# Eight of 28 row blocks of a down product moved from TensorE to ScalarE and GpSimd, and four weight loads asked for eight steps earlier

## Chip, cores and metric

One core of a Trainium2 chip. The metric is the device time of one execution in microseconds (us). The three timed runs of the kernel before took 263.06, 263.49 and 263.74 us; their median, 263.49 us, is the time to compare with. About 0.3% (0.79 us) is what a measurement of this kernel can tell from no change.

## The reference

The output mixes two branches of one input `x` (2048 tokens of 1024 columns, bf16) by a gate per token.

```python
g = sigmoid((x * gate_w).sum(-1, keepdims=True))
# branch a: linear attention, 32 heads of 32 columns, over all tokens
q, k, v = split(x @ wqkv)
phi(z)  = concat(softmax(z @ w_phi), softmax(-(z @ w_phi)))     # per head
kv, z   = sum over tokens of phi(k)^T v,  and of phi(k)
a       = (phi(q) kv / (phi(q) z + 1e-6)) @ wo
# branch b: one expert, for one token only
idx     = argmax over tokens of x @ w_r
y       = (silu(x[idx] @ w_gate) * (x[idx] @ w_up)) @ w_down    # 1024 -> 3584 -> 1024
b       = x, with y * sigmoid(r[idx]) added to row idx
out     = g * a + (1 - g) * b
```

The last product of branch b, (1 x 3584) @ (3584 x 1024), is the down product. 3584 rows are 28 blocks of 128.

## The kernel before

TensorE works through three stages. First v of all 16 token tiles, with the folding of `w_phi` into the k and q weights. Then a loop of steps `i`: steps 0 to 31 are the key stage, one half of the heads of one token tile a step (`feats` computes pk, two exponentials on ScalarE, `ssum` and its reciprocal `rq` on VectorE, the product `phi` on GpSimd, and `k_kv`, five steps later, adds to `kvps`). Steps 32 to 63 (NU = 32) are the query stage: `feats` gives `pq` and `phi`; `q_turn` transposes `phi` by DMA into `phT`; `q_num` later multiplies it with KV (`num`), and VectorE divides (`rden`, `o_sb`); `q_oT` transposes by DMA into `oT`; `q_wo` later multiplies by `wo` (`po`), and VectorE combines with `xg` into `oo`, which is stored. How much later is set by a running count of TensorE's time, `pe`: a step takes what is due.

The one token of branch b is worked in between. Its weights pass through SBUF in 1 MB buffers: "A" is one of three in the pool `ring`, "D" one of two in `shp`, "W" and "V" halves of a tile in `wob`, "X" and "Y" halves of one in `w16`. The up and gate products take four passes r (`ffn_gu`): passes 0 and 1 at step 14, passes 2 and 3 at step 22. `gu_load` asks for a buffer of weights; in pass 1 each buffer takes two DMAs, a gate part of 768 KB and an up part of 256 KB. Pass 0 is asked for at step 0 (`gu0`), the others where they are used. At steps 4 and 7 `qfold_turn` issues four DMA transposes each (`wqf` from `wfT`); the `ring` buffer of the first `wfT` is the one that the last buffer of pass 1 takes over.

At step 38 (DN) `ffn_down` loads the down weights (seven chunks of four row blocks) and issues 56 matmuls into one PSUM bank, `yps`: 28 blocks times two column halves, in four column groups of 32 that run side by side. `moe_cols` copies the bank out and gathers four rows into `y4` (8 x 2 x 128) by four small DMAs. `moe_sum` (step 44) adds the two parts on GpSimd into `y2`, `moe_scale` (46) scales it, `moe_out` (47) writes it to DRAM (`ydr`), and `moe_spread` (57), held to program order, reads it back broadcast over 128 partitions (`ybc`). Tiles 14 and 15 add `ybc` in `q_xg`; for the others `add_row` adds the row in DRAM.

A compiler puts instructions in order on each engine and in each DMA queue, by the program's order and by what it holds to be ready; what is wrapped in `keep_in_program_order` stays in the order written. Each engine then runs its list in order.

Of the kernel before, what the change touches and what calls it, by code (L numbers as in the profile page):

```python
# [9 lines left out]
F32 = mybir.dt.float32  # L10
I32 = mybir.dt.int32
U32 = mybir.dt.uint32
ALU = mybir.AluOpType
ACTF = mybir.ActivationFunctionType
AX = mybir.AxisListType
# [3 lines left out]
P = 128  # L19
# [15 lines left out]
VC = [0, 256, 640, 1026]  # L35
VW = 1026
TOH = 14
TX = 4
KFOLDS = {5: (0, 3), 7: (3, 3), 9: (6, 2)}
PACKS = {(13, 2): (0, 0), (14, 1): (1, 0), (15, 0): (0, 1), (15, 2): (1, 1)}  # L40
# [130 lines left out]
def kernel(  # L171
# [74 lines left out]
    nc.gpsimd.iota(iot[:, 0:NT], pattern=[[1, NT]], base=0, channel_multiplier=0, allow_small_or_imprecise_dtypes=True)  # L246
    nc.gpsimd.iota(iot[:, NT:NT + 1], pattern=[[0, 1]], base=0, channel_multiplier=1, allow_small_or_imprecise_dtypes=True)
    hh = const.tile([P, NFB], BF, name="hh")

    small_ps = psS.tile([P, 512], F32, name="small_ps")  # L250
    ffn_ps = small_ps[:, 0:64]
# [272 lines left out]
        return w  # L524

    def ffn_gu(r, bufs):
        ws = moe.pop("gu0", None) or [gu_load(r, k, b) for k, b in enumerate(bufs)]
        acc = psB.tile([P, 512], F32, name="facc", tag="pB")
        for k, w in enumerate(ws):
            for q in range(2):  # L530
                for g in range(4):
                    kb = 4 * k + 2 * q + g // 2 if r == 3 else 2 * k + q
                    nc.tensor.matmul(acc[32 * g:32 * g + 32, :], lhsT=xs32[:, kb, :],  # L533
                                     rhs=w[:, (q * 4 + g) * 512:(q * 4 + g + 1) * 512], start=(k == 0 and q == 0),
                                     stop=(k == len(ws) - 1 and q == 1),
                                     tile_position=(0, 32 * g), skip_group_check=True)
        gs = wk.tile([P, 512], F32, name="gs", tag="junk", bufs=2)
        nc.scalar.copy(out=gs[:], in_=acc[:])
        g0 = 16 * r
        step = 4 if r >= 1 else 1  # L540
        for g in range(0, 4, step):
            nc.sync.dma_start(out=gT[g0 + 4 * g:g0 + 4 * (g + step), :], in_=gs[32 * g:32 * (g + step):32, :])

    def ffn_down(c0, c1):
        if c0 == 0:
            moe["wd"] = [wd_load(c, p) for c, p in enumerate("AAADDWV")]
            moe["yps"] = psB.tile([P, 512], F32, name="yps", tag="pB")
        ws = moe["wd"]
        for blk in range(4 * c0, 4 * c1):
            for n in range(2):  # L550
                g = (blk % 2) * 2 + n
                nc.tensor.matmul(moe["yps"][32 * g:32 * g + 32, :], lhsT=hh32[:, blk, :],  # L552
                                 rhs=ws[blk // 4][:, blk % 4, n * 512:(n + 1) * 512], start=(blk < 2),
                                 stop=(blk >= NFB - 2), tile_position=(0, 32 * g), skip_group_check=True)

    def moe_cols():
        ym = ring.tile([P, D * 2], F32, name="ym", tag="wch")
        ys = ym[:, 0:512]
        y4 = ym[0:KB, 512:768].rearrange("p (s c) -> p s c", s=2)
        ybc = ym[:, 1280:1792].bitcast(BF)  # L560
        moe["ybc"] = ybc
        nc.scalar.copy(out=ys, in_=moe["yps"][:])
        for g in range(4):
            nc.sync.dma_start(out=y4[4 * (g % 2):4 * (g % 2) + 4, g // 2, :], in_=ys[32 * g:32 * g + 1, :])
        moe["y4"] = y4

    def moe_sum(tick):
        y4 = moe["y4"]
        y2 = const.tile([KB, P], BF, name="y2")
        moe["y2"] = y2  # L570
        nc.gpsimd.tensor_copy(out=y2[0:1, 0:1], in_=tick)
        nc.gpsimd.tensor_tensor(out=y2[:], in0=y4[:, 0, :], in1=y4[:, 1, :], op=ALU.add)

    def moe_scale(tick):
        y2 = moe["y2"]
# [228 lines left out]
    GU = (14, 22)  # L804
    TU = 29
    DN = NU + 6
    TF, TNUM, TWO, TKV = 1.73, 0.27, 1.73, 0.27
    L_NUM0, N_1, L_NUM1, L_NUM, L_WO0, L_WO, MOST = 11.0, 6, 17.0, 11.5, 8, 6, 2
    pe = 0.0
# [4 lines left out]
    while i < 2 * NU or n_next < NU or wos:  # L814
        if i in GU:
            r = 2 * GU.index(i)
            ffn_gu(r, 'WVAD')
            ffn_gu(r + 1, ('DXYA', 'AA')[r // 2])
        if i == DN - 3:
            nc.scalar.copy(out=hh32[0:1, 0, 0:1], in_=moe["e"][0:1, 0, 1, 0:1])  # L820
            nc.scalar.copy(out=hh32[:], in_=hh[:].unsqueeze(2).to_broadcast([P, NFB, 32]))
        if i == 19:
            moe["wo"] = w16.tile([P, KB, D], BF, name="wo_sb", tag="w16")
            nc.gpsimd.tensor_copy(out=moe["wo"][0:1, 0, 0:1], in_=kst[i - 1][0:1, 0, 0, 0:1])
            nc.sync.dma_start(out=moe["wo"][:], in_=A_wo.rearrange("(kb p) n -> p kb n", p=P))
        if i == DN:
            ffn_down(0, 7)
            moe_cols()
            qp["oo"] = wob.tile([P, 16, 512], BF, name="oo", tag="wo")
            qp["n_oo"] = 0  # L830
            qp["late"] = []
        if LAG <= i < NU + LAG:
            k_kv(i - LAG)
            pe += TKV
        if i < NU:
            kst[i] = feats(i, wkf, False)
        if i == NU:
            qp["phT"] = wfp.tile([P, 8, NPU, P], BF, name="phT", tag="wf")
        if i == NU + LAG - 1:
            kv_finish()  # L840
            kscope.close()
            kvscope.close()
            psN = main.enter_context(tc.tile_pool(name="psN", bufs=1, space=PSUM))
            qp["num"] = [psN.tile([P, 2 * 512], F32, name="num%d" % h_) for h_ in range(2)]
            qp["qw"] = main.enter_context(tc.tile_pool(name="qw", bufs=2))
        if NU <= i < 2 * NU:
            q_turn(i - NU, feats(i - NU, wqf, True))
            pe += TF
            fend[i - NU] = pe
        if i == 0:  # L850
            moe["gu0"] = [gu_load(0, k, b) for k, b in enumerate("WVAD")]
        if i < 4:
            kv_zero(i)
        if i == 2:
            gates()
        if i in (QT0, QT1):
            h = 4 * (i == QT1)
            nc.scalar.copy(out=wqf[0:1, 0, h * P:(h + 4) * P:P], in_=moe["e"][0:1, 0, 0, 0:4])
            for a in range(h, h + 4):
                qfold_turn(a)  # L860
        if i == TU:
            ffn_turn()
            ffn_mid()
        if i == 0:
            route_row()
        if i == 10:
            xs_turn()
        if i == 16:
            one_hot()
        if i == 19:  # L870
            one_hot_cols()
        if i == 23:
            one_hot_sums()
        if i == NU + 18:
            one_hot_row()
        if i == DN + 6:
            moe_sum(moe["rs"][0:1, 0:1])
        if i == DN + 8:
            moe_scale(moe["rs"][0:1, 0:1])
        if i == DN + 9:  # L880
            moe_out()
        if i == DN + 19:
            moe_spread()
        late = i >= 2 * NU
        for k in range(MOST if not late else 1):
            if n_next >= NU or n_next not in fend or pe < fend[n_next] + (L_NUM0 if n_next < N_1 else max(L_NUM, L_NUM1 - 1.5 * max(0, n_next - 26))):
                break
            q_num(n_next)
            pe += TNUM
            nend[n_next] = pe  # L890
            if n_next % 2 == 1:
                q_oT(n_next // 2)
                wos += [(n_next // 2, 0), (n_next // 2, 1)]
            n_next += 1
            if n_next == NU:
                range_flag()
                flag_in = 1
        wo_at = nend[2 * wos[0][0] + 1] + (L_WO if wos[0][0] else L_WO0) if wos else 1e9
        if late and pe < wo_at:
            pe = min(wo_at, fend[n_next] + L_NUM if n_next < NU else 1e9)  # L900
        if pe >= wo_at:
            t, nh = wos.pop(0)
            if nh == 0:
                q_xg(t)
            q_store(0 if late else 1)
            q_wo(t, nh, late and nh == 1)
            if t == NT - 1:
                q_store(0)
            if (t, nh) == (NT - 2, 1):
                tc.mark_branch_hint_location("general", engines=[ET.PE])  # L910
            pe += TWO
            if n_next == NU:
                flag_in -= 1
                if flag_in == 0:
                    range_flag_end()
            if (t, nh) == (TOH - 1, 1):
                q_store(0)
                add_row(moe["y2c"][:, 0, :], nc.values_load(moe["ixu"][0:1, 0:1], engines=[ET.Pool], min_val=0,
                                                            max_val=TOH * P - 1))
        i += 1  # L920
# [40 lines left out]
```

## Time and profile before

| | |
|---|---|
| median of the timed runs | 263.49 us |
| the profiled execution | 264.23 us |
| its span, first to last instruction | 262.6 us |
| TensorE (PE) busy | 256.4 us |
| VectorE (DVE) busy | 175.4 us |
| GpSimd (POOL) busy | 128.1 us |
| ScalarE (ACT) busy | 127.6 us |
| clock granted to TensorE | 0.999 of full speed |

The durations below come from the profiled execution, which took 0.74 us more than the median; its span leaves out 1.63 us around the first and the last instruction. A line such as "L552 PE MATMUL yps<-wch,hh x56" reads: line 552 of the kernel, engine, operation, what is written from what, how many. Matmuls are pipelined, and the profile models where one ends, so the distance from the first matmul of a group to the first of the next is the better measure of what a group takes.

### The profile page before, as it was taken

To read this page: it belongs to the slowest core of one execution; us is meant where nothing else is said; L and a number is where in the kernel's file an instruction comes from. 1 tells how busy PE (TensorE), PEld (TensorE's weight loads), DVE (VectorE), ACT (ScalarE), POOL (GpSimd) and SP (SyncE) were. 2 spreads that over 40 slices of the span, in tenths; PEclk is the share of its full clock that TensorE was granted. 3 is DMA by queue.
4 is the path that set the end of the run, shared out by engine and by line. 5 is a ranking of instruction groups with operands and counts; after the bars stand their busy time and mean duration, and the time that the engine had idled before them with its cause. 6 is when DMAs were issued, how large, how long until landed. Compare 5 with 4: busy or idle time off the path is not lost.

```text
span 262.6 us, 5420 instructions
## 1 busy us (share of the span) xinstructions
PE 256.4 (98%) x2039; PEld 137.9 (53%) x2062; DVE 175.4 (67%) x310; ACT 127.6 (49%) x262; POOL 128.1 (49%) x87
## 2 busy tenths in 40 slices
PE   7999999999999999999999999999999999999995
PEld 3666666665445545545555455445444444445543
DVE  3020221015879855998798769899799797888973
ACT  3043555447575544545556667447344553435220
POOL 6000000000079995779989868665535545455001
PEclk9999999999999999999999999999999999999999
DMA  6979999988999889969995998999977899999962
GB/s 203 279 129 176 167 198 150 196 122 309 408 384 182 192 210 386 401 199 391 386 387 184 195 151 178 236 169 250 250 168 155 171 180 177 206 190 206 141 164 83
DMA packets 111082, 58.48 MB, mean 223 GB/s; under 512 B 93692, under 2 KB 98892, under 8 KB 111052
## 3 DMA queue, kind: packets, MB, share of 16 engines
q1 hardware_dynamic: 108364, 53.77, 85.8%
q10 hardware_dynamic: 2656, 4.33, 6.9%
q8 instruction: 17, 0.28, 0.5%
q14 instruction: 13, 0.11, 0.2%
q0 software_dynamic: 32, 0.00, 0.1%
HBM read 31.27 MB, written 4.23 MB: 135 GB/s over the span
## 4 chain that ended last, share of the span: by engine, by line
PE 96%; DMA 2%; issue 1%; SPq 0%; DVE 0%
PE pq L645 21%; PE pk L645 21%; PE po L747 21%; PE pv L599 19%; PE kvps L675 3%; PE num L708 3%; PE facc L533 3%; DMA wv_sb<-in_A_wqkv_dram 2%; PE vbank L616 1%; PE pv L616 1%; PE yps L552 1%; PE vbank L323 1%; PE vbank L340 1%; SPq L273 0%; PE pW L323 0%
## 5 line engine op out<-in xcount | busy, mean ns | idle before, releaser
L662 POOL TENSOR_TENSOR phi<-e,rq 128x1024 bf16<-128x1024 bf16 x64 | 121.4, 1912 | 61.7 <-DVE rq L659 36.0
L655 DVE TENSOR_REDUCE ssum<-e 128x32 f32<-128x1024 bf16 x64 | 77.4, 1210 | 14.3 <-ACT e L651 14.0
L645 PEld LDWEIGHTS <-xT 128*128 128x128 bf16 x512 | 47.4, 98 | 51.9 <-issue 0.7
L645 PE MATMUL pq<-wqf,xT 128*128 128x512 bf16 x256 | 60.3, 379 | 0.0
L645 PE MATMUL pk<-wkf,xT 128*128 128x512 bf16 x245 | 59.2, 379 | 0.6
L747 PE MATMUL po<-wo_sb,oT 128*128 128x512 bf16 (+2 forms) x252 | 58.1, 372 | 0.6
L599 PE MATMUL pv<-wv_sb,xT 128*128 128x256 bf16 (+2 forms) x336 | 50.0, 307 | 0.0
L599 PEld LDWEIGHTS <-xT 128*128 128x128 bf16 x336 | 32.0, 97 | 16.3 <-issue 0.5
L607 ACT CAST v_all<-pv 128x384 bf16<-128x384 f32 (+1 forms) x45 | 20.1, 451 | 34.9 <-PE pv L599 25.7
L747 PEld LDWEIGHTS <-oT 128*128 128x128 bf16 x264 | 24.0, 98 | 23.9 <-issue 0.2
L650 ACT ACTIVATE e<-pq 128x512 bf16<-128x512 f32 x32 | 18.9, 592 | 34.2 <-PE pq L645 34.2
L650 ACT ACTIVATE e<-pk 128x512 bf16<-128x512 f32 x32 | 19.1, 597 | 26.3 <-PE pk L645 22.1
L475 POOL COPY wch<-shv 1x1 bf16<-1x1 bf16 x3 | 0.4, 177 | 53.4 <-DMA shv<-in_A_wqkv_dram 53.4
L751 DVE SCALAR_TENSOR_TENSOR oo<-po,gate,xg 128x512 bf16<-128x512 f32 (+2 forms) x33 | 23.8, 722 | 3.6 <-PE po L747 3.5
L659 DVE RECIPROCAL rq<-ssum 128x32 f32<-128x32 f32 x64 | 22.2, 347 | 1.3
L713 DVE TENSOR_TENSOR o_sb<-num,rden 128x512 bf16<-128x512 f32 x32 | 21.7, 679 | 0.7
L328 DVE CAST wkf<-vbank 128x512 bf16<-128x512 f32 x6 | 3.9, 686 | 25.2 <-PE vbank L323 25.2
L651 ACT ACTIVATE e<-pk 128x512 bf16<-128x512 f32 x32 | 18.9, 591 | 0.0
L651 ACT ACTIVATE e<-pq 128x512 bf16<-128x512 f32 x32 | 18.9, 590 | 0.0
L732 ACT ACTIVATE xg<-xin,omg 128x1024 f32<-128x1024 bf16 x16 | 18.4, 1148 | 0.5
L346 DVE CAST wfT<-vbank 128x512 bf16<-128x512 f32 x9 | 5.8, 681 | 16.5 <-PE pW L340 16.5
L675 PEld LDWEIGHTS <-phi 128*128 128x128 bf16 x256 | 12.0, 98 | 7.3 <-issue 0.8
(137 smaller groups left out, 154.0 us busy)
## 6 DMA issues: line engine op xcount, KB each, us to landing
wch<-in_B_w_down_dram SPq DMA_DIRECT2D x7, 1024.0 KB
wch<-in_B_w_up_dram SPq DMA_DIRECT2D x6, 1024.0 KB
wch<-in_B_w_gate_dram SPq DMA_DIRECT2D x4, 1024.0 KB
xin<-in_A_x_dram ACTq DMA_DIRECT2D x16, 256.0 KB
out_dram<-oo SPq DMA_DIRECT2D x31, 128.0 KB
wch<-in_B_w_gate_dram SPq DMA_DIRECT2D x4, 768.0 KB
wv_sb<-in_A_wqkv_dram SPq DMA_DIRECT2D x8, 256.0 KB
wo_sb<-in_A_wo_dram SPq DMA_DIRECT2D x1, 2048.0 KB
```

Source lines behind the costliest of these rows:

```text
L599: nc.tensor.matmul(pv[:, 0:hi - lo], lhsT=xT[:, kb, t * P:(t + 1) * P], rhs=wv_sb[:, kb, lo:hi], start=(kb == 0), stop=(kb == KB - 1))
L607: copy(out=v_all[:, t, h0:h1, 0:DH], in_=pv[:, 0:(h1 - h0) * DH].rearrange("p (h d) -> p h d", d=DH))
L645: nc.tensor.matmul(pk[:].rearrange("p (c r) f -> p c r f", r=4) if is_q else pkf, lhsT=xT[:, kb, t * P:(t + 1) * P], rhs=q_heads(wf, kb, h ...
L650: nc.scalar.activation(out=e[:, :, 0, :], in_=pk[:], func=ACTF.Exp)
L651: nc.scalar.activation(out=e[:, :, 1, :], in_=pk[:], func=ACTF.Exp, scale=-1.0)
L655: nc.vector.tensor_reduce(out=ssum[:], in_=e2, axis=AX.X, op=ALU.add)
L659: nc.vector.reciprocal(out=rs, in_=ssum[:])
L662: nc.gpsimd.tensor_tensor(out=phi[:].rearrange("p h s f -> p (h s) f"), in0=e2, in1=_bc(rs, [P, HH * 2, DH]), op=ALU.mult)
L675: nc.tensor.matmul(kv_slot(pr), lhsT=phi[:, 2 * pl:2 * pl + 2, :, :].rearrange("p h s f -> p (h s f)"), rhs=v_all[:, t, hf * HH + 2 * pl:h ...
L713: nc.vector.tensor_tensor(out=st["o"][:, hf * HH:(hf + 1) * HH, :].rearrange("p (r h) d -> p r h d", h=2), in0=nv[:, :, :, 0:DH], in1=rden ...
L747: nc.tensor.matmul(po[:, 0:w], lhsT=st["oT"][:, kb, :], rhs=moe["wo"][:, kb, sl], start=(kb == 0), stop=(kb == KB - 1))
L751: qp["gated"] = nc.vector.scalar_tensor_tensor(out=o_out[:, 0:w], in0=po[:, 0:w], scalar=gate[:, t:t + 1], in1=st["xg"][:, sl], op0=ALU.mu ...
```

## The change

Eight of the 28 blocks of the down product, chunks 1 and 2, are no longer multiplied on TensorE. `down_part` runs from step 44 on, one or two parts a step, sixteen in all (eight blocks times two column halves): ScalarE multiplies a 128x512 piece of the weights by the block's column of `hh` (kept in f32 as `hhf`), and from the third part on GpSimd adds the piece into an f32 accumulator `acc` of 128x1024. At step 56 `down_cols` sums `acc` over its partitions on VectorE with a transpose in blocks of 32, a reduction and a second transpose; at step 57 four DMAs put the four partial sums next to the two from TensorE. `moe_sum` moves from GpSimd to VectorE and from step 44 to 59, `moe_scale` from 46 to 60, `moe_out` from 47 to 61, `moe_spread` from 57 to 63. The loads of the down weights come in another order and other buffers: chunks 0, 3, 4, 5, 6 for TensorE first, then 1 and 2. The loads of pass 1 of the up and gate weights are written at step 6 instead of step 14.

```diff
+PW = (1, 2)
+    hhf = const.tile([P, NFB], F32, name="hhf")
     def ffn_gu(r, bufs):
-        ws = moe.pop("gu0", None) or [gu_load(r, k, b) for k, b in enumerate(bufs)]
+        ws = moe.pop("gu%d" % r, None) or [gu_load(r, k, b) for k, b in enumerate(bufs)]
...
-    def ffn_down(c0, c1):
-        if c0 == 0:
-            moe["wd"] = [wd_load(c, p) for c, p in enumerate("AAADDWV")]
-            moe["yps"] = psB.tile([P, 512], F32, name="yps", tag="pB")
-        ws = moe["wd"]
-        for blk in range(4 * c0, 4 * c1):
+    def ffn_down():
+        moe["wd"] = {c: wd_load(c, p) for c, p in zip((0, 3, 4, 5, 6) + PW, "ADDWVAA")}
+        moe["yps"] = psB.tile([P, 512], F32, name="yps", tag="pB")
+        blks = [b for b in range(NFB) if b // 4 not in PW]
+        for blk in blks:
             for n in range(2):
                 g = (blk % 2) * 2 + n
                 nc.tensor.matmul(moe["yps"][32 * g:32 * g + 32, :], lhsT=hh32[:, blk, :],
...
+    def down_part(n):
+        b, half = divmod(n, 2)
+        blk = 4 * PW[b // 4] + b % 4
+        if n == 0:
+            moe["acc"] = qp["qw"].tile([P, D], F32, name="acc", tag="acc", bufs=1)
+        o = moe["acc"][:, half * 512:(half + 1) * 512]
+        w = moe["wd"][PW[b // 4]][:, b % 4, half * 512:(half + 1) * 512]
+        to = o if b == 0 else qp["qw"].tile([P, 512], F32, name="prod", tag="prod", bufs=2)[:]
+        tc.keep_in_program_order(nc.scalar.activation(out=to, in_=w, func=ACTF.Copy, scale=hhf[:, blk:blk + 1]))
+        if b:
+            tc.keep_in_program_order(nc.gpsimd.tensor_tensor(out=o, in0=to, in1=o, op=ALU.add))
+
+    def down_cols():
+        tr = ring.tile([P, D * 2], F32, name="tr", tag="wch")
+        tc.keep_in_program_order(nc.vector.transpose(out=tr[:, 0:D], in_=moe["acc"][:]))
+        nc.vector.tensor_reduce(out=tr[:, D:D + 32], in_=tr[:, 0:D].rearrange("p (c i) -> p c i", i=32), axis=AX.X, op=ALU.add)
+        nc.vector.transpose(out=tr[:, D + 32:D + 64], in_=tr[:, D:D + 32])
+        moe["part"] = tr[:, D + 32:D + 64]
+
+    def down_gather():
+        for q in range(4):
+            nc.sync.dma_start(out=moe["y4"][:, 2 + q, :], in_=moe["part"][32 * q:32 * q + 32, :])
...
-        nc.gpsimd.tensor_copy(out=y2[0:1, 0:1], in_=tick)
-        nc.gpsimd.tensor_tensor(out=y2[:], in0=y4[:, 0, :], in1=y4[:, 1, :], op=ALU.add)
+        nc.vector.tensor_copy(out=y2[0:1, 0:1], in_=tick)
+        with nc.allow_low_precision(reason="fp32 sum, rounded once"):
+            nc.vector.tensor_reduce(out=y2[:], in_=y4.rearrange("p s c -> p c s"), axis=AX.X, op=ALU.add)
...
+    DP = DN + 6
...
             nc.scalar.copy(out=hh32[:], in_=hh[:].unsqueeze(2).to_broadcast([P, NFB, 32]))
+            nc.scalar.copy(out=hhf[:], in_=hh[:])
...
+        if i == QT1 - 1:
+            moe["gu1"] = [gu_load(1, k, b) for k, b in enumerate("DXYA")]
...
-        if i == DN + 6:
+        if DP <= i < DP + 11:
+            for n in range((i - DP) * 3 // 2, (i - DP + 1) * 3 // 2):
+                down_part(n)
+        if i == DP + 12:
+            down_cols()
+        if i == DP + 13:
+            down_gather()
+        if i == DP + 15:
             moe_sum(moe["rs"][0:1, 0:1])
-        if i == DN + 8:
+        if i == DP + 16:
             moe_scale(moe["rs"][0:1, 0:1])
-        if i == DN + 9:
+        if i == DP + 17:
             moe_out()
-        if i == DN + 19:
+        if i == 2 * NU - 1:
             moe_spread()
```

## Rows read from the trace of the kernel before

**Rows 1.** The page, part 1: span, and TensorE's busy time.
```profile
span 262.6 us, 5420 instructions
...
PE 256.4 (98%) x2039; PEld 137.9 (53%) x2062; DVE 175.4 (67%) x310; ACT 127.6 (49%) x262; POOL 128.1 (49%) x87
```

**Rows 2.** All that TensorE's matmuls waited for: us in total, times, longest us.
```profile
PE small_ps L207 <- PEq L945: 1.1, 1, 1.1
PE vbank L616 <- DMA wv_sb<-in_A_wqkv_dram: 0.8, 1, 0.8
```

**Rows 3.** Two stretches: length, busy us (instructions) of PE, PEld, DVE, ACT, POOL; clock, DMA.
```profile
168.00:210.00 42.00, 41.74 (x280) 20.85 (x284) 37.31 (x65) 20.13 (x37) 21.93 (x14) 1.00 0.93 197
...
212.00:238.00 26.00, 25.84 (x167) 12.73 (x168) 21.51 (x37) 11.93 (x22) 14.01 (x8) 1.00 0.97 183
```

**Rows 4.** Instructions in time, down product on TensorE: start us, length us, which.
```profile
147.76 3.21 PE L552 MATMUL yps<-wch,hh 128*32 128x512 bf16 x56
150.90 1.47 PE L645 MATMUL pq<-wqf,xT 128*128 128x512 bf16 x6
```

**Rows 5.** Instructions in time, up and gate passes on TensorE.
```profile
93.40 4.01 PE L533 MATMUL facc<-wch,xs 128*32 128x512 bf16 x64
...
96.82 0.10 PEld L533 LDWEIGHTS <-xs 128*32 128x32 bf16 x4 [0.50 <-issue]
...
97.34 0.43 PE L675 MATMUL kvps<-v_all,phi 128*128 128x66 bf16 x8
...
113.32 2.77 PE L533 MATMUL facc<-wch,xs 128*32 128x512 bf16 x48
...
116.02 0.43 PE L675 MATMUL kvps<-v_all,phi 128*128 128x66 bf16 x8
```

**Rows 6.** Instructions in time, SyncE's queue ahead of the first passes.
```profile
85.97 0.41 SPq L509 DMA_DIRECT2D wch<-in_B_w_gate_dram  x1
86.49 7.00 SPq L349 DMA_TRANSPOSE wqf<-wfT  x4
93.54 2.81 SPq L509 DMA_DIRECT2D wch<-in_B_w_up_dram  x3
```

**Rows 7.** Groups by line and shape: count | busy us, mean ns of one | idle before.
```profile
L662 POOL TENSOR_TENSOR phi<-e,rq 128x1024 bf16<-128x1024 bf16 x64 | 121.4, 1912 | 61.7 <-DVE rq L659 36.0 <-ACT e L651 12.5 <-DVE rden L712 5.7
L655 DVE TENSOR_REDUCE ssum<-e 128x32 f32<-128x1024 bf16 x64 | 77.4, 1210 | 14.3 <-ACT e L651 14.0
...
L732 ACT ACTIVATE xg<-xin,omg 128x1024 f32<-128x1024 bf16 x16 | 18.4, 1148 | 0.5
...
L572 POOL TENSOR_TENSOR y<-ym 8x128 bf16<-8x128 f32 x1 | 0.4, 446 | 0.1
...
L571 POOL CAST y<-rq 1x1 bf16<-1x1 f32 x1 | 0.2, 176 | 0.0
```

**Rows 8.** Instructions in time, VectorE and TensorE around step 50.
```profile
191.26 0.74 DVE L751 SCALAR_TENSOR_TENSOR oo<-po,gate,xg 128x512 bf16<-128x512 f32 x1
...
192.65 1.67 DVE L450 TENSOR_TENSOR ixm<-ixm,ixf 1x1 f32<-1x1 f32 x1
...
194.42 0.23 DVE L712 RECIPROCAL rden<-num 128x16 f32<-128x16 f32 x1
...
196.42 1.89 PE L747 MATMUL po<-wo_sb,oT 128*128 128x512 bf16 x7
```

**Rows 9.** Instructions in time: an output transpose, and the matmuls that read it.
```profile
222.43 1.24 SPq L723 DMA_TRANSPOSE oT<-o_sb  x1
...
237.21 1.67 PE L747 MATMUL po<-wo_sb,oT 128*128 128x512 bf16 x7
```

**Rows 10.** Instructions in time: gather, last query transpose, reader of the spread row.
```profile
155.70 2.95 SPq L564 DMA_DIRECT2D ym<-ym  x4
...
243.21 1.24 SPq L692 DMA_TRANSPOSE phT<-phi  x1
...
247.73 1.28 DVE L734 SCALAR_TENSOR_TENSOR xg<-ym,oh,xg 128x1024 f32<-128x1024 bf16 x1
```

More of the change, by code (lines that the diff above doesn't have):

```diff
@@ L552, in ffn_down @@
                 nc.tensor.matmul(moe["yps"][32 * g:32 * g + 32, :], lhsT=hh32[:, blk, :],
-                                 rhs=ws[blk // 4][:, blk % 4, n * 512:(n + 1) * 512], start=(blk < 2),
-                                 stop=(blk >= NFB - 2), tile_position=(0, 32 * g), skip_group_check=True)
+                                 rhs=moe["wd"][blk // 4][:, blk % 4, n * 512:(n + 1) * 512], start=(blk < 2),
+                                 stop=(blk in blks[-2:]), tile_position=(0, 32 * g), skip_group_check=True)
+    def down_part(n):
[18 more added lines that the diff above has]
+            nc.sync.dma_start(out=moe["y4"][:, 2 + q, :], in_=moe["part"][32 * q:32 * q + 32, :])
     def moe_cols():
@@ L558, in moe_cols @@
         ys = ym[:, 0:512]
-        y4 = ym[0:KB, 512:768].rearrange("p (s c) -> p s c", s=2)
+        y4 = ym[0:KB, 512:1280].rearrange("p (s c) -> p s c", s=6)
         ybc = ym[:, 1280:1792].bitcast(BF)
@@ L826 @@
         if i == DN:
-            ffn_down(0, 7)
+            ffn_down()
             moe_cols()
```

## The prediction

> **What bounds the kernel now.** I read the page's first part, then what TensorE waited for, then the stretches of the stage that the change loads. TensorE is busy for 256.4 of the 262.6 us span [rows 1], and its waits for others come to 1.9 us, both at the start [rows 2]. So a matmul taken off it is worth its time, and work on another engine costs nothing until TensorE has to wait for it. From 168 to 210 us VectorE is busy 37.3 of 42 us, ScalarE 20.1 and GpSimd 21.9 [rows 3]: VectorE is the one with little room.
>
> **The down product.** The 56 matmuls of `yps` begin at 147.76 us, the next `pq` at 150.90 [rows 4]: 3.14 us, 56.1 ns each. The change leaves 40 (16 of 56 go, two per block). Four neighbouring column groups stay in the same rotation, since the blocks that go are an even count in a row. Saved: 16 x 56.1 ns = **0.90 us**, straight from the path. The seven loads keep their size; only the order and the buffers change, and the two chunks for ScalarE sit in two `ring` buffers until used.
>
> **The experts' second weights.** The 64 matmuls of passes 0 and 1 begin at 93.40 us and are followed by `kvps` at 97.34: 3.94 us. The 48 of passes 2 and 3 take 113.32 to 116.02: 2.70 us, 56.25 ns each. At that rate 64 take 3.60, so 0.34 us is a stall, and the weight loads stand still before the last four of them at 96.82 [rows 5]. The reason is in SyncE's queue: the gate part of the last buffer of pass 1 is asked for at 85.97, then come four transposes of `wqf` from 86.49 to 93.49, and only then the up part of the same buffer (the first of three at 93.54) [rows 6]. Nothing in TensorE's list of waits names it [rows 2], because a matmul in flight is drawn busy until its modelled end. With the load written at step 6, ahead of those transposes (step 7), both parts should go at about 86 us. The transposes then come one issue (about 0.5 us) later; what they write is first read by `pq` in the query stage, which begins six steps ahead of the down product at 147.76 [rows 4], so some 40 us hide it. Gain: between 0 (the compiler's order keeps the up part behind the transposes) and 0.34 us; I take **0.34**, because the gate part already overtook those transposes with a later step number.
>
> **ScalarE's products.** 16 multiplications of 128x512 bf16 into f32. Not in the trace; the nearest is `xg`, the same operation on 1024 columns, 1148 ns [rows 7]. Between half of it and all of it; I take 0.6 us: 9.6 us in all, against 21.9 us that ScalarE is free in the stretch [rows 3]. On the path: 0.
>
> **GpSimd's sums.** 14 f32 additions of 128x512 (the first product of each half goes straight into `acc`). Nearest rows: `phi`, 1912 ns for 1024 columns; the small sum `y`, 446 ns for 128 columns of two f32 inputs; and 176 ns for a single element [rows 7]. By columns of `phi` one addition takes 0.96 us. From `y`, (446 - 176) / 128 = 2.1 ns a column, it takes 512 x 2.1 + 176 = 1.26 us. By bytes of `phi` (2 KB read and 2 KB written per partition in 1.74 us, where the addition reads 4 KB and writes 2) it takes 2.8 us. I take 1.26, the one row of the same kind: 14 x 1.26 = 17.6 us. GpSimd is free for 42 - 21.9 = 20.1 us in the stretch, and the two `y` instructions that leave it give 0.6 more: it fits, at 95% of the engine. The end at 2.8 us is a rival below.
>
> The Trainium skill, page "GPSIMD Engine Reference", section "Elementwise — side-by-side cycle accounting", speaks against putting such additions on GpSimd and gives 4497 ns for 2048 f32 columns. Scaled to 512 columns that is an estimate of 1.12 us, 15.7 us for all; by that page the sum above would be the same, and the price by bytes would be out.
>
> What hides a late GpSimd: it runs `phi`, whose transpose is consumed far later. The same distance shows in the output: the eleventh `oT` transpose is issued at 222.43 us and the po group that reads it (the 21st of 32) begins at 237.21 [rows 9]. So delays of a few us on either chain reach nobody. The short distances are buffers: one `oo` ends at 192.0 and the `po` after next begins at 196.42 [rows 8], 4.4 us of slack; the two `pq` buffers, freed by ScalarE's exponentials, turn in the same rhythm, with about as much.
>
> A wait is added on ScalarE: each product waits for the addition two before it (two `prod` buffers), and the next exponentials queue behind it, for which `pq` waits. It holds TensorE only once GpSimd is more than those 4.4 us behind.
>
> **VectorE's new work, steps 56 to 59 (about 209 to 226 us).** A 128x1024 f32 transpose, a reduction of 1024 columns, a 32-column transpose, a 768-column reduction in place of GpSimd's sum. Nearest row: `ssum`, 1024 columns in 1210 ns [rows 7]. I take 1.2 + 1.2 + 0.1 + 0.9 = 3.4 us; 2.2 if the transpose costs nothing, 4.6 if it costs double. VectorE is free for 26 - 21.5 = 4.5 us between 212 and 238 [rows 3]. The trace has such a burst already: at step 50 four `ixm` instructions (1.67 us the longest) push the next `rden` to 194.42 with no idle time ahead of it, and the `po` at 196.42 begins on time [rows 8]. The burst at step 56 is some 0.4 us longer and comes at the same place in the rhythm. On the path: 0, up to 1.2 us if the dear end meets a late gather.
>
> **SyncE's queue.** The gather at step 57 adds four small DMAs. The four of `moe_cols` took 2.95 us of issue [rows 10]; behind them stand `phT`, `oT` and stores, with the distances above. Row `ydr` is written at step 61 instead of 47. The spread moves from step 57 to 63 and, pinned, comes after the last `phT` at 243.21; its consumer in VectorE's order stands at 247.73 [rows 10]. That leaves some 3 us for 256 KB: tight, but the two tiles that read the result close only the last four of 32 outputs. On the path: 0 to 0.5 us. The extra copy `hhf` lies on ScalarE ahead of the query stage: nothing.
>
> **Sum.** The profiled execution took 264.23 us (span 262.6 and 1.63 around it), 0.74 above the median of 263.49. 264.23 - 0.90 - 0.34 = 262.99; on the median, 263.49 - 1.24 = **262.25 us**.
>
> **Rivals.**
> (a) The order of the loads does not change what TensorE sees: the up part stays behind the transposes. Then only the down product counts: 263.49 - 0.90 = 262.6 us. For it: the order on SyncE is the compiler's, and it mixed the steps before. Against: the new step number is below that of the transposes.
> (b) The new work at the end of the query stage collides: VectorE's dear end, a sum that waits at the head of its queue for the gather, and the late spread cost TensorE 0.5 to 1.2 us: 262.75 to 263.45 us. For it: VectorE has 4.5 us left for 3.4. Against: 4.4 us of slack at the buffers, and the burst at step 50.
> (c) Slower: GpSimd's additions go by bytes, 2.8 us each. 14 x 2.8 = 39.2 us against 20.7 free: 18.5 us too many; the buffers swallow 4.4, the rest reaches TensorE by way of ScalarE: 263.49 - 1.24 + 14.1 = 276 us. It loses more than 0.3% once an addition takes over 1.94 us (14 x 1.94 = 27.1 = 20.7 + 4.4 + the gain of 1.24 + 0.8). Against: by bytes the small `y` sum would take 0.73 us, and it takes 0.45.
>
> **How the numbers follow.** Forecast 0.62, (a) 0.15, (b) 0.17, (c) 0.06. 0.3% is 0.79 us, about what a measurement of this kernel can tell from no change: faster means below 262.70. The forecast holds there with some 0.59 of its 0.62 (three runs of before lie within 0.43 of their median), (a) with 0.09 of its 0.15; (b) is nearly all within 0.3%. So faster 0.68, same 0.25, slower 0.07. Low end: the forecast less the spread of runs, 261.85; high end: the dear end of (b), 263.4; what is left out is (c) and edges.
>
> **What would show it.** Right: 40 `yps` matmuls in 2.25 us; passes 0 and 1 in 3.60 us, with both parts of the last buffer issued next to each other near 86 us; `po` and `pq` at 3.71 us a pair through 168 to 238 us; POOL near 95% busy from 168 to 205. Wrong: a wait of TensorE for VectorE or ScalarE anywhere after 165 us, additions over 1.9 us, or the exponentials waiting behind products.

## The result and the profile after

The changed kernel is slower: 267.4 us (266.95 to 268.14) against 263.69 us for the kernel before in runs beside it, ratio 1.0132, 95% interval 1.0101 to 1.0162. The prediction was 262.25 us, faster. Its profiled execution took 267.97 us, with a span of 266.3.

Read first what the forecast promised. Page of the changed kernel, part 1 (answers [rows 1]):

```profile
PE 256.9 (96%) x2046; PEld 137.6 (52%) x2046; DVE 176.7 (66%) x315; ACT 137.8 (52%) x279; POOL 144.6 (54%) x99
```

Instructions in time on TensorE, changed kernel: start us, length us (answers [rows 4, 5]):

```profile
93.66 3.64 PE L535 MATMUL facc<-wch,xs 128*32 128x512 bf16 x64
97.23 0.43 PE L700 MATMUL kvps<-v_all,phi 128*128 128x66 bf16 x8
...
147.65 2.34 PE L553 MATMUL yps<-wch,hh 128*32 128x512 bf16 x40
149.92 1.25 PE L670 MATMUL pq<-wqf,xT 128*128 128x512 bf16 x5
```

The down product takes 149.92 - 147.65 = 2.27 us in place of 3.14, passes 0 and 1 take 97.23 - 93.66 = 3.57 in place of 3.94. Both gains are there in this pair of traces, 1.24 us; that the second was there to be won only in some executions is said below. The loss is in the list of TensorE's waits (answers [rows 2]; us in total, times, longest us):

```profile
PE num L733 <- DVE o_sb L738: 1.8, 1, 1.8
PE po L772 <- DMA oT<-o_sb: 1.7, 1, 1.7
PE small_ps L208 <- PEq L981: 1.1, 1, 1.1
PE vbank L641 <- DMA wv_sb<-in_A_wqkv_dram: 1.0, 1, 1.0
PE num L464 <- DVE o_sb L738: 0.2, 1, 0.2
PE kvps L700 <- POOL phi L687: 0.2, 1, 0.2
```

Two single waits are new, 1.8 and 1.7 us. Where they lie is seen in time (changed kernel, 240 to 252 us, TensorE, SyncE and VectorE):

```profile
240.20 0.42 PE L733 MATMUL num<-KV,phT 128*128 128x66 bf16 x8
...
243.40 0.68 DVE L738 TENSOR_TENSOR o_sb<-num,rden 128x512 bf16<-128x512 f32 x1
...
244.14 0.41 PE L733 MATMUL num<-KV,phT 128*128 128x66 bf16 x8 [1.80 <-DVE o_sb L738]
...
245.20 1.24 SPq L717 DMA_TRANSPOSE phT<-phi  x1
...
246.49 0.66 SPq L613 DMA_DIRECT2D ym<-ydr  x1
...
247.24 1.24 SPq L748 DMA_TRANSPOSE oT<-o_sb  x1
...
249.82 0.42 PE L733 MATMUL num<-KV,phT 128*128 128x66 bf16 x8
251.14 1.28 DVE L759 SCALAR_TENSOR_TENSOR xg<-ym,oh,xg 128x1024 f32<-128x1024 bf16 x1 [1.76 <-DMA ym<-ydr]
251.95 1.90 PE L772 MATMUL po<-wo_sb,oT 128*128 128x512 bf16 x8 [1.71 <-DMA oT<-o_sb]
...
254.03 0.22 PE L464 MATMUL num<-ident,nbb 128*128 128x128 bf16 x1 [0.18 <-DVE o_sb L738]
```

The same instructions in the kernel before, in the same order:

```profile
240.91 0.42 PE L708 MATMUL num<-KV,phT 128*128 128x66 bf16 x8
242.89 0.42 PE L708 MATMUL num<-KV,phT 128*128 128x66 bf16 x8
...
244.54 1.29 SPq L723 DMA_TRANSPOSE oT<-o_sb  x1
...
248.58 0.42 PE L708 MATMUL num<-KV,phT 128*128 128x66 bf16 x8
248.84 1.89 PE L747 MATMUL po<-wo_sb,oT 128*128 128x512 bf16 x8
250.60 0.22 PE L462 MATMUL num<-ident,nbb 128*128 128x128 bf16 x1
```

Take the first `facc` of the experts (93.40 before, 93.66 after) as the zero of both, since the start of an execution varies. At the `num` of 240.20 the changed kernel is 0.97 us ahead. From there to the next `num` it takes 3.94 us where the kernel before takes 1.98: 1.96 lost. From 249.82 to the `num` of L464 it takes 4.21 in place of 2.02: 2.19 lost. Behind that the two are equal: the last `po` ends 8.87 us later in both. -0.97 + 1.96 + 2.19 = 3.18; the stretch from the first `facc` to the end of the last `po` measures 169.24 us in place of 166.07, 3.17 more. So the whole loss lies in two places of the last 26 us; 0.27 of the promised 1.24 had been lost before.

The chain that ended last passes through both places (start us, us; changed kernel):

```profile
240.90 1.22 DVE ssum L680
...
243.28 1.90 POOL phi L687
...
245.20 1.24 SPq L717
...
246.49 4.55 DMA ym<-ydr
...
251.14 1.28 DVE xg L759
```

VectorE is late with its work, then the spread of the row, 4.55 us from its issue to its landing, stands in the chain.

### The profile page after: what moved, and what is told of

The parts are those of the page before. It is cut to its first block, busy times and chain, and to the rows that moved or that the text cites. A ratio compares the mean times of both kernels' runs of the same rounds, so it can differ in the third digit from the quotient of the medians.

```text
span 266.3 us, 5434 instructions
## 1 busy us (share of the span) xinstructions
PE 256.9 (96%) x2046; PEld 137.6 (52%) x2046; DVE 176.7 (66%) x315; ACT 137.8 (52%) x279; POOL 144.6 (54%) x99
## 4 chain that ended last, share of the span: by engine, by line
PE 61%; DVE 17%; ACT 7%; DMA 6%; POOL 3%; issue 3%; SPq 1%; ACTq 0%; POOLq 0%; DVEq 0%
PE pv L624 18%; PE pk L670 17%; PE pq L670 10%; DVE ssum L680 8%; PE po L772 5%; PE kvps L700 3%; DVE oo L776 3%; DMA mrow<-mi 2%; PE facc L535 2%; POOL phi L687 2%; ACT e L676 2%; DVE o_sb L738 2%; ACT e L675 2%; DMA wv_sb<-in_A_wqkv_dram 2%; DMA ym<-ydr 2%
## 5 line engine op out<-in xcount | busy, mean ns | idle before, releaser
L772 PE MATMUL po<-wo_sb,oT 128*128 128x512 bf16 (+2 forms) x264 | 59.6, 372 | 1.8 <-DMA oT<-o_sb 1.7
L670 PE MATMUL pk<-wkf,xT 128*128 128x512 bf16 x256 | 59.8, 379 | 0.0
L567 POOL TENSOR_TENSOR acc<-prod,acc 128x512 f32<-128x512 f32 x14 | 17.6, 1273 | 0.0
L733 PEld LDWEIGHTS <-phT 128*128 128x128 bf16 x256 | 12.1, 98 | 9.0 <-issue 2.1
```

The lines of the kernel that those rows point to most:

```text
L670: nc.tensor.matmul(pk[:].rearrange("p (c r) f -> p c r f", r=4) if is_q else pkf, lhsT=xT[:, kb, t * P:(t + 1) * P], rhs=q_heads(wf, kb, h ...
L772: nc.tensor.matmul(po[:, 0:w], lhsT=st["oT"][:, kb, :], rhs=moe["wo"][:, kb, sl], start=(kb == 0), stop=(kb == KB - 1))
```

## The experiments

Each kernel is built on the kernel before or on the changed one, as the diff says. "Stretch" is the first `facc` to the end of the last `po` in the one profiled execution (before 166.07 us, of which 0.37 is the stall of passes 0 and 1, which is not in every execution, so 165.70 without it; after 169.24). The ratio is to runs of the kernel before on the same chip.

**Twenty blocks and nothing else** (kernel before; eight blocks are left out of the sum).

```diff
-        for blk in range(4 * c0, 4 * c1):
+        for blk in [x for x in range(NFB) if x // 4 not in (1, 2)]:
```

> The kernel before with only 20 of the 28 row blocks of the down product multiplied (chunks 1 and 2 are loaded and left out of the sum), and nothing else. It gives the direct gain by itself: 40 matmuls of yps in 2.25 us, no new wait, 0.9 us less than before (about 262.8 against 263.7). If TensorE's time there were not on the path, the time would stay.

Measured: 262.93 us, ratio 0.997 [0.995, 0.999], stretch 164.84, no new wait. The gain of the down product is real: 0.70 us by the medians, against 0.86 of shorter `yps` (3.14 to 2.28); the stretch is shorter by the same 0.86 than the 165.70 without the stall.

**The loads alone** (kernel before).

```diff
+        if i == QT1 - 1:
+            moe["gu1"] = [gu_load(1, k, b) for k, b in enumerate("DXYA")]
```

> The kernel before with one edit: the weight loads of pass 1 written at step 6. If the up part was what stalled TensorE, the 64 matmuls of passes 0 and 1 take 3.60 us from the first to the next kvps (3.94 before), and the time falls by 0.34 us, to about 263.15 against 263.5. If the stall had another cause, 3.94 us stay and the time stays.

Measured: 264.39 us against 263.72, ratio 1.0024 [0.9998, 1.0049]. Passes 0 and 1 take 3.57 us, as hoped; passes 2 and 3 take 4.01 us in place of 2.70. SyncE's queue, then TensorE:

```profile
85.65 0.41 SPq L509 DMA_DIRECT2D wch<-in_B_w_gate_dram  x1
86.13 1.12 SPq L509 DMA_DIRECT2D wch<-in_B_w_up_dram  x1
87.36 7.22 SPq L349 DMA_TRANSPOSE wqf<-wfT  x4
96.58 1.43 SPq L509 DMA_DIRECT2D wch<-in_B_w_up_dram  x2
...
101.38 0.97 SPq L509 DMA_DIRECT2D wch<-in_B_w_up_dram  x2
...
116.03 0.62 PE L533 MATMUL facc<-wch,xs 128*32 128x512 bf16 x8 [1.12 <-DMA wch<-in_B_w_up_dram]
```

The up part now goes before the transposes of `wqf`. These start at 87.36 in place of 86.49 [rows 6], and the up loads that follow go later at first: at 96.58 and, after five small DMAs, from 101.38 on, where the kernel before issues the same from 95.47 and from 99.71 on. Pass 3 waits 1.12 us for one of them. A stall is gone in one place and there in another. With the loads at step 6 passes 2 and 3 took 2.70 to 2.71 us in three traces and 2.93, 3.36 and 4.01 in three others; with the loads at step 14 they took 2.70 to 2.71 in all eight. How the earlier loads bring the stall about is not shown. The load that pass 3 waits for is the last of the four, issued at 104.81 us, which the kernel before issues at 104.63; by the chain that ends in that wait it lands 11.17 us later. In the changed kernel without the sums (below) the last load goes 10.81 us behind the first `facc`, sooner than in the kernel before (11.23), and pass 3 waits for it all the same. So a late issue is not enough of a reason.

**The late spread alone** (kernel before, same data, issued at step 63 instead of 57).

```diff
-        if i == DN + 19:
+        if i == 2 * NU - 1:
```

> The kernel before with one edit: the broadcast of the row over 128 partitions moved from step 57 to step 63. Theory A (the late broadcast costs by itself: its 256 KB lie ahead of the output transposes of the last tiles in the DMA queue, and VectorE waits for it at the head of its list): 1.5 to 2 us more, with a wait of a late po for its oT transpose of over 1 us. Theory B (VectorE is late by then, for other reasons, and the broadcast only looks bad in the changed kernel): within 0.4 us of before, no such wait.

Measured: 265.41 us, ratio 1.0063 [1.0024, 1.0102], stretch 167.28. The waits behind it are the second of the two above:

```profile
244.34 0.66 SPq L588 DMA_DIRECT2D ym<-ydr  x1
245.09 1.24 SPq L723 DMA_TRANSPOSE oT<-o_sb  x1
...
249.12 1.28 DVE L734 SCALAR_TENSOR_TENSOR xg<-ym,oh,xg 128x1024 f32<-128x1024 bf16 x1 [1.47 <-DMA ym<-ydr]
250.06 1.90 PE L747 MATMUL po<-wo_sb,oT 128*128 128x512 bf16 x8 [1.22 <-DMA oT<-o_sb]
```

One line, moved six steps, costs 1.2 us of stretch (1.6 against the 165.70 without the stall) and 1.7 by the medians: the `oT` transpose issued right behind it is late for its `po`. Its own time in the queue is the usual 1.24 us; what is late is its landing. `po` gets it 4.97 us after its issue. None of the sums is in this kernel.

**The changed kernel without the spread** (zeros are added to the last two tiles instead of the row).

```diff
-        if i == 2 * NU - 1:
-            moe_spread()
+        if i == DN + 1:
+            nc.gpsimd.memset(moe["ybc"], 0.0)
```

> The changed kernel without the broadcast: the row that tiles 14 and 15 add is set to zero instead, so the expert's row is left out of the last two tiles. Theory A: the wait of po for oT (1.71 us) and of VectorE for the row (1.76 us) go, the wait of num for o_sb (1.80 us) stays; 267.4 falls to about 265.3. Theory B (VectorE and GpSimd late): the oT is late all the same, and less than 0.7 us is gained.

Measured: 265.69 us, ratio 1.0082 [1.0054, 1.011]. The wait of `po` falls from 1.7 to 0.4 us, the wait of `num` for `o_sb` stays at 1.8, and the stretch is 168.17 us. The two are separate. The `oT` that the spread delayed is issued at 246.09 here and read on time at 249.64, 3.55 us later, where the changed kernel needed 4.71 (247.24 to 251.95).

**The changed kernel without the sums** (only the first product of each half is made; 7 of 8 blocks are missing).

```diff
-            for n in range((i - DP) * 3 // 2, (i - DP + 1) * 3 // 2):
+            for n in range((i - DP) * 3 // 2, min(2, (i - DP + 1) * 3 // 2)):
```

> The changed kernel with only parts 0 and 1 of 16, so 14 of the 16 weight pieces are left out of the sum (14 products on ScalarE and 14 additions on GpSimd gone); the transpose, the reductions, the gather and the late broadcast stay. Theory C (the additions hold up the products on ScalarE, these the exponentials, these VectorE, which so enters the end 2 us late): the wait of num for o_sb goes, 267.4 falls by 2 us or more, to 265.4 or less. Theory D (VectorE's own new 4 us alone make it late): 267.4 falls by less than 0.7 us and the wait of num for o_sb stays at over 1 us.

Measured: the wait of `num` is gone, that of `po` is 1.2 us, pass 3 waits 0.5 us for its weights. The time, 266.47 us (264.59 to 269.02), ratio 1.0092 [1.0059, 1.0125], fell by less than the trace says: the traced execution took 265.91 us, and its stretch of 167.11 is 2.13 shorter than the changed kernel's, but the ten times scatter over 4.4 us. The trace decides the question of the wait; that the time falls by the 2 us that were expected is not shown.

**The changed kernel without VectorE's columns** (no transposes, reduction and gather of `acc`; its share is missing from the row).

```diff
-        if i == DP + 12:
-            down_cols()
-        if i == DP + 13:
-            down_gather()
```

> The changed kernel without VectorE's transposes and reduction of acc and without the gather (products and additions stay; their sum is left out of the result). If GpSimd's and ScalarE's new work alone make VectorE late, the wait of num for o_sb stays near 1.8 us and less than 0.7 us is gained. If it takes both, the wait goes and 1.5 us or more is gained (267.4 to 265.9 or less), the po that waits for its oT behind the late broadcast staying at over 1 us.

Measured: 265.83 us, ratio 1.0118 [1.0059, 1.0178], an interval that holds the changed kernel's 1.0132; there were four runs, three of them between 264.62 and 266.43 and one of 268.93, so the times settle nothing. The trace: `num` still waits for `o_sb`, 0.5 us in place of 1.8, and `po` 1.2; the stretch is 167.04, 2.20 shorter than the changed kernel's. So the whole wait of `num` needs both, a VectorE that was held up and a VectorE that has more to do.

**Four product buffers in place of two.** The products are bf16 here, so that four buffers take the room of two in f32, and the additions read bf16: number of buffers and type change together.

```diff
-        to = o if b == 0 else qp["qw"].tile([P, 512], F32, name="prod", tag="prod", bufs=2)[:]
+        to = o if b == 0 else qp["qw"].tile([P, 512], BF, name="prod", tag="prod", bufs=4)[:]
```

> The changed kernel with four product buffers in bf16 instead of two in f32 (the same room). ScalarE's products then no longer wait for GpSimd's additions (9.8 us of such waits in the changed kernel). If that wait is what makes VectorE late at the end, the wait of num for o_sb (1.80 us) falls below 0.6 us and the time falls by 1.2 us or more, to about 266. If ScalarE's added work itself (16 products of 0.72 us) or VectorE's new work makes it late, the wait stays over 1.2 us and so does the time.

Measured: 265.3 us, ratio 1.0053 [1.0026, 1.0079], stretch 166.39. The wait of `num` is gone, the wait of `po` is 1.2 us. How the two buffers cost something is read on ScalarE, VectorE and GpSimd. Changed kernel, 204 to 209 us:

```profile
205.00 0.72 ACT L565 ACTIVATE prod<-wch,hhf 128x512 f32<-128x512 bf16 x1 [1.91 <-POOL acc L567]
205.63 0.58 ACT L675 ACTIVATE e<-pq 128x512 bf16<-128x512 f32 x1
206.10 0.59 ACT L676 ACTIVATE e<-pq 128x512 bf16<-128x512 f32 x1
206.72 1.22 DVE L680 TENSOR_REDUCE ssum<-e 128x32 f32<-128x1024 bf16 x1 [1.24 <-ACT e L676]
206.78 2.51 POOL L567 TENSOR_TENSOR acc<-prod,acc 128x512 f32<-128x512 f32 x2
```

The product waits 1.91 us for the addition that frees its buffer, the two exponentials stand behind it in ScalarE's order, and VectorE's `ssum` idles 1.24 us for them. All such waits of the changed kernel together:

```profile
DVE ssum L680 <- ACT e L676: 21.2, 28, 4.0
...
ACT prod L565 <- POOL acc L567: 9.8, 8, 2.2
```

In the kernel before `ssum` waited 14.0 us for `e` [rows 7]; with four buffers it waits 16.0, and no product waits. Two buffers in bf16 were not run, but the trace with four speaks for the number of buffers: eight of the twelve products behind the first two start 0.94 to 2.34 us before the addition two before them ends, and with two buffers they would have had to wait for it; the type makes an addition only 0.11 us shorter. Nearly all of the difference lies where the products are made: from 168 to 212 us `ssum` waited 1.5 us for `e` in the kernel before, 7.8 in the changed one and 2.0 with four buffers. What that does to VectorE, in two stretches (length, then busy us and instructions of PE, PEld, DVE, ACT, POOL; clock, DMA share, GB/s). Changed kernel:

```profile
168.00:212.00 44.00, 44.00 (x301) 21.82 (x299) 35.51 (x65) 29.69 (x51) 37.65 (x25) 1.00 0.93 192
212.00:238.00 26.00, 25.90 (x168) 12.71 (x167) 24.66 (x43) 11.08 (x22) 13.76 (x8) 1.00 0.89 174
```

With four buffers:

```profile
168.00:212.00 44.00, 44.00 (x301) 21.90 (x300) 37.67 (x68) 29.66 (x52) 37.34 (x27) 1.00 0.94 198
212.00:238.00 26.00, 26.00 (x170) 12.72 (x168) 24.34 (x42) 12.27 (x25) 13.44 (x8) 1.00 0.81 166
```

TensorE is never idle from 168 to 212 us in either. But VectorE gets 35.51 us of its work done there in the one and 37.67 in the other: 2.2 us are put off. (The kernel before, without the new work, gets 39.28 us done from 168 to 212, so four buffers give back a part, and it is enough.) In the next stretch VectorE is full at 24.66 of 26 us and can't make them up. So it comes late into the last pieces, where TensorE waits for it.

**The row and its spread earlier** (changed kernel with four buffers, the loads back at step 14, `ydr` written at step 60, the spread at 61).

```diff
-        if i == DP + 17:
+        if i == DP + 16:
             moe_out()
-        if i == 2 * NU - 1:
+        if i == DP + 17:
             moe_spread()
```

> The changed kernel with the pass 1 loads back at step 14, four bf16 product buffers, the row written at step 60 and broadcast at step 61. If the late broadcast and the products waiting on additions are the two causes, both waits of TensorE at the end go and 262.6 to 263.2 us remain (the 0.9 us gain against 263.7). If VectorE's new work still makes it late, the wait of num for o_sb stays at over 1 us and the time lies at or above 264.

Measured: 265.45 us, ratio 1.0061 [1.0033, 1.0088]. The wait of `po` falls to 0.2 us, and another takes its place:

```profile
236.70 0.66 SPq L613 DMA_DIRECT2D ym<-ydr  x1
...
239.76 3.99 SPq L717 DMA_TRANSPOSE phT<-phi  x1
...
246.11 0.43 PE L733 MATMUL num<-KV,phT 128*128 128x66 bf16 x8 [2.17 <-DMA phT<-phi]
```

The transpose 3 us behind the spread occupies the queue for 3.99 us where others take 1.24. Two steps earlier the spread is no longer late for its reader, but a transpose behind it is late for its own. That the spread is what held it for so long is likely from the order and not shown: the kernel with the same buffers and loads and no spread (below) has none of over 1.30 us from 230 to 248 us, but long ones occur without a spread ahead too (last section).

**All three suspects taken out, the sums kept** (changed kernel with four buffers, loads at step 14, and zeros in place of the row as above).

> The changed kernel with all three suspects taken out and the new sums kept: the experts' second loads back at step 14, four bf16 product buffers, and the broadcast of the row left out (zeros are added instead). Theory 'three separate causes' (A broadcast, B two product buffers, C loads): none of the three waits is left, the time is that of the kernel with 20 blocks and no sums, 262.8 to 263.2 us, ratio about 0.997. Rival 'the added work itself is too much for ScalarE and GpSimd': a lag of 1 us or more stays at num(29) or later, and the time stays above 264.3.

Measured: 262.99 us against 263.81, ratio 0.9974 [0.9949, 0.9999], stretch 164.88. All that TensorE waited for:

```profile
PE small_ps L208 <- PEq L979: 1.1, 1, 1.1
PE vbank L641 <- DMA wv_sb<-in_A_wqkv_dram: 0.7, 1, 0.7
```

These are the two waits of the start [rows 2]. All 14 additions, 16 products and VectorE's columns are in this kernel: the work itself costs TensorE nothing.

**Four blocks, with the row ready in time** (products of chunk 1 only, four buffers, loads at step 14, spread at step 57 as before). Chunk 2 goes back to TensorE and the loads are ordered for it. Columns, gather, sum, scale and `moe_out` move to 7, 8, 10, 11 and 12 steps after `DP`.

```diff
-PW = (1, 2)
+PW = (1,)
...
-        if i == 2 * NU - 1:
+        if i == DN + 19:
             moe_spread()
```

> 4 of 28 blocks by ScalarE and GpSimd instead of 8 (8 products, 6 additions), four bf16 product buffers, loads at step 14, so that the row is ready early enough for its broadcast at step 57 as in the kernel before. Theory 'what costs is the broadcast among the last transposes': nothing late at the end of the query stage, gain of 8 matmuls x 56.1 ns = 0.45 us, time about 263.2 us (262.9 to 263.5), ratio about 0.998. Rival 'any such work in the query stage costs': num or po waits again and the time is 264 to 265.

Measured: 263.43 us against 263.81, ratio 0.9996 [0.9974, 1.0018], stretch 165.44, no wait of `num`, `kvps` or `po`. The median moved by 0.38 us, near the 0.45 expected, but the interval holds no change too.

**Six blocks, begun two steps sooner, spread at step 57** (four buffers, loads at step 14; `DP` is `DN + 4`, columns at 10 steps after it, gather 11, sum 13, scale and `moe_out` 14).

```diff
-        blks = [b for b in range(NFB) if b // 4 not in PW]
+        blks = [b for b in range(NFB) if not 4 <= b < 10]
...
-    DP = DN + 6
+    DP = DN + 4
...
-        if DP <= i < DP + 11:
+        if DP <= i < DP + 8:
...
-        if i == 2 * NU - 1:
+        if i == DN + 19:
             moe_spread()
```

> 6 of 28 blocks by ScalarE and GpSimd (12 products, 10 additions), begun two steps sooner, four bf16 product buffers, loads at step 14, broadcast at step 57 as in the kernel before. Theory 'work that is done before the last transposes costs nothing': gain of 12 matmuls x 56.1 ns = 0.67 us, no new wait of num, kvps or po, stretch from the first facc to the last po 0.7 to 1.0 us shorter than before's 166.07 us, time about 263.0 us against 263.7, ratio 0.9975. Rival: VectorE's transposes of acc at step 52 wait for GpSimd's last addition and hold up the exponentials' sums, some 1 us at a num wait, ratio 1.001 or more.

Measured: 263.09 us (262.24 to 263.71) against 263.81, ratio 0.997 [0.9949, 0.9991], stretch 165.05, TensorE's waits again only those of the start. It leaves nothing out and is faster than the kernel before by 0.3%, and so than the changed one; its products are rounded to bf16 before they are added. Blocks, start, buffers, loads and spread are all other than in the changed kernel, so which of them it takes is not told by this run.

**The changed kernel with only the loads back at step 14.**

```diff
-        if i == QT1 - 1:
-            moe["gu1"] = [gu_load(1, k, b) for k, b in enumerate("DXYA")]
```

> The changed kernel with only the loads of pass 1 back at step 14. Theory 'the loads edit moves a stall, 0 to 0.3 us won in pass 1 and 0 to 1.3 us lost in passes 2 and 3': time the same as the changed kernel's or up to 0.9 us better, 266.5 to 267.4; num waits 1.8 us and po 1.7 us as before. Rival 'the loads are worth 0.34 us': 0.3 us slower, 267.7.

Measured: 266.71 us, ratio 1.0121 [1.0083, 1.0159], `num` waits 1.8 us and `po` 1.3. The loads are not what made the changed kernel slow; whether they cost the few tenths that the medians differ is within the intervals.

## Why the prediction was wrong, step by step

**Down product: right.** 0.90 us predicted, 0.87 in the trace, and alone it gave 0.70 by the medians.

**Loads: half right.** The order of issue came as predicted (gate at 86.28, up at 86.75) and passes 0 and 1 took 3.57 us against 3.60. What failed is that the step ended there. It asked who reads what the delayed transposes write (`pq`, 40 us later), and not what becomes of the loads behind them: in three of the six traces with the loads at step 6 pass 3 stalls, by 0.23 to 1.31 us, in none of the eight others. By what path is open. Also, the 0.34 us was read from one execution: of the seven other traces with the loads at step 14, six show 3.56 to 3.58 us for the two passes and one 3.74. There was little to win.

**Prices of the new work: within their bounds.** Products took 722 ns (0.6 us predicted), additions 1273 ns (1.26 us):

```profile
L567 POOL TENSOR_TENSOR acc<-prod,acc 128x512 f32<-128x512 f32 x14 | 17.6, 1273 | 0.0
L565 ACT ACTIVATE prod<-wch,hhf 128x512 f32<-128x512 bf16 x14 | 10.1, 722 | 9.8 <-POOL acc L567 9.8
```

VectorE's four: 1.18, 1.19, 0.20 and 1.48 us, 4.05 in all where 3.4 was taken, within the bounds of 2.2 to 4.6. GpSimd was less full than forecast: by the prediction's own terms (21.9 - 0.6 + 17.6) / 42 is 93%, not 95, and it was busy for 30.65 of the 37 us from 168 to 205, 83%. The Trainium skill, page "GPSIMD Engine Reference", section "Elementwise — side-by-side cycle accounting", has 4497 ns for 2048 f32 columns, from which the prediction's estimate for the addition was 1.12 us; the trace has 1.27 for f32, 1.16 with one bf16 input. Rival (c), 2.8 us by bytes, is out.

**"It holds TensorE only once GpSimd is more than those 4.4 us behind": this step failed.** It followed the wait of a product to `pq` and stopped, since TensorE did not wait there, and in fact it did not until 242 us. It did not follow it to VectorE, the engine that the same text had named as the one with little room. The exponentials that stood behind a product came late to `ssum` (7.8 us of waits from 168 to 212 us in place of 1.5), and at least 2.2 us of VectorE's work slid from that stretch into the one that the next paragraph filled with new work. The free 4.5 us of VectorE between 212 and 238 us [rows 3] were counted once, for the 3.4 us of new work, although something else had to go there as well. Shown by the kernel without the sums and the one with four buffers (wait of `num` gone in both) and by the kernel without columns (1.8 falls to 0.5). Two of the signs of being wrong that the prediction had named came with it: exponentials waiting behind products, and TensorE waiting for VectorE.

**"So delays of a few us on either chain reach nobody": this step failed too.** The distance of 14.8 us between an `oT` and its `po` [rows 9] was taken from 222 us and used for the whole stage. At the end it is short: in the kernel before the `oT` issued at 244.54 is read at 248.84, 4.3 us later. In the changed kernel it is issued at 247.24, behind a late `phT` and the spread, and read at 251.95.

**SyncE's queue: the place was right, the price was not, and half of the mechanism was missing.** "Some 3 us for 256 KB: tight" and 0 to 0.5 us. The spread took 4.55 us to land, its reader waited 1.76 us. But TensorE's wait is for the transpose behind it, which the step didn't ask for: it followed the spread to its reader and not the queue behind the spread. Moved alone, it costs 1.2 to 1.6 us of stretch. In the changed kernel, which is already late there, 2.19 us are lost in that place; 0.33 of them stay without the spread (249.39 to 251.74 in place of 2.02 us), so 1.86 are the spread's.

**Rival (b)** named the place, the late end of the query stage, and VectorE and the spread as the cause. It gave 0.5 to 1.2 us, where 4.15 were lost. Its size was wrong for the reason above: the slacks that were to absorb it were those of the middle of the stage.

Open are the time of the kernel without sums, which fell by less than its trace says, and the path from the earlier loads to the stall of pass 3. The number of product buffers and their type were changed together, and only the trace speaks for the number as what removed the wait of `num`.

## What to carry to other kernels

A slack read in the middle of a pipelined stage does not hold at its end, where the distances between producer and reader run out; read it at the place where the new work lands. When an added wait stands at the head of an engine's queue, follow what is behind it to the engine with the least free time, not only to the one that bounds the kernel: work that such an engine puts off comes due later, together with whatever else was planned for that room. A transfer that is moved has two costs, its own lateness and that of every transfer queued behind it; here six of the eight blocks, with four buffers and with the loads and the spread at their old steps, gained 0.3%.

## What the runs showed of the hardware

A 256 KB broadcast from a 32 KB source took 4.55 us from issue to landing among the other transfers (4.69 in the kernel with the late spread alone). The transpose issued right behind it took its usual 1.24 us of the queue, but landed late: its reader got it 4.71 and 4.97 us after its issue in those two, where without the spread 3.55 us were enough. The transpose issued some 3 us behind the spread held SyncE's queue for 3.99 us in the kernel with the early row. At step 57 that place shows less: 2.26 us in the kernel before (spread at 221.68, `phT` at 224.43), 1.34 to 2.73 in the four others with the spread there, and 1.24 where the spread was moved away. But transposes of over 2 us occur without a spread ahead as well: the kernel with the late spread has one of 3.26 at 229.55 us, 15 us before its spread. Whether the transfer engines or the queue cause it, the runs don't tell.

An addition on GpSimd with one bf16 input and one in f32 took 1164 ns for 128x512, with both in f32 1273 ns; the product's output type made no difference to ScalarE (721 and 722 ns).
